# Which side of a subtraction is strided: the read or the write

## The chip, the cores and the metric

The kernel runs on one core of one Trainium2 chip. The metric is the device time of one execution in microseconds. Engines: TensorE (PE; its weight loads are PEld), VectorE (DVE), ScalarE (ACT), GpSimd (POOL), SyncE (SP, which only issues DMAs here).

## The reference

Attention over 8 batches, 8 heads, 576 tokens and 64 dimensions (a pooled part and a band of neighbours), followed by a dense layer. Only the dense layer matters here:

```python
def _moe_ref(x, w_in, w_out):          # x: 4608 x 512, w_in: 512 x 2048, w_out: 2048 x 512
    h = x @ w_in
    g = h - np.tanh(h)
    return (g @ w_out).astype(np.float32)
```

## The kernel before

One batch gives one block of 576 tokens. Its attention result lies in `xT` (features on partitions), with the tokens of a batch ordered as c, then g: token 4g + c, four classes c of G = 144. The dense layer takes the first 128 g of each c, so 512 tokens, as a block (`mm1`): 16 chunks of 128 hidden features, each four matmuls into one PSUM bank (line 782), tanh on ScalarE into the f32 tile `u` (line 794) and the subtraction on VectorE into the bf16 tile `gT` (line 797).

The last 16 g of each c, 64 tokens a batch, are the left tokens. They are done for two batches at once, four times in all (`left1(m, e)`, m = 0 to 3), in four groups e of four feature chunks: 16 matmuls of 128 columns each fill one PSUM bank (line 809); its 512 columns are, from outer to inner, chunk f (4), batch b (2), c (4) and g (16). Then tanh into `u` (line 820, the same order) and the subtraction into `gL` (line 822). `gL[:, f, :]` has 128 columns in the order of the tokens, b, g, c, since `left2` uses it as stationary operand (line 835) and stores its result in rows of tokens. So somewhere between the bank and `gL`, c and g change places, and the subtraction does it.

`u` is a ring of three buffers, and a bank or a buffer is free again when the subtraction has read it. `second` makes the second product (line 1003), which needs sums over `gT` that VectorE makes (line 938, the token sums); lines 691 (mask), 723 and 741 are VectorE's part of the attention of later batches, lines 491 to 562 bring q and k into their layouts: line 496 copies a transposed k out of PSUM with a changed order of elements, line 501 a transposed q in the same order, line 551 and line 557 pick q (and k) of a few tokens out of `rT`, line 562 reorders k inside SBUF. Line 410 casts v.

All instructions are put in one order written out by hand (`TURNS`), from which each engine's queue follows; an engine works its queue in order. Costs given to `op` (such as the 690 in line 822) change nothing in that order.

Of the kernel before, what the change touches and what calls it, by code (L numbers as in the profile page):

```python
# [10 lines left out]
ALU = mybir.AluOpType  # L11
# [3 lines left out]
class Plan:  # L15
# [13 lines left out]
    def op(self, eng, ns, fn, reads=(), writes=(), port=False, opens=None, uses=(),  # L29
           choice=None, rows=128, share=0.4):  # L30
        i = len(self.ops)
        deps = set()
        for key in reads:
            if key in self.last_write:
                deps.add(self.last_write[key])
        for key in writes:
            if key in self.last_write:
                deps.add(self.last_write[key])
            deps.update(self.readers.get(key, ()))
        for key in reads:  # L40
            self.readers.setdefault(key, set()).add(i)
        for key in writes:
            self.last_write[key] = i
            self.readers[key] = set()
        deps.discard(i)
        if opens and not isinstance(opens, list):
            opens = [opens]
        names = set(uses) | {o[0] for o in opens or ()}
        if choice:
            letter = self.engines[self.choices]  # L50
            self.choices += 1
            eng, ns, fn, port = next(a[:4] for a in choice if a[0][0] == letter)
        self.ops.append((fn, deps, opens or (), names))
        return i
# [34 lines left out]
def kernel(  # L89
# [125 lines left out]
    def fixed(name, shape, dt, n=None, pool=const):  # L215
        if n is None:
            return pool.tile(shape, dt, name=name, tag=name)
        return [pool.tile(shape, dt, name=f"{name}{i}", tag=f"{name}{i}")
                for i in range(n)]
# [39 lines left out]
    u = fixed("u", [128, 512], FP32, 3)  # L259
# [7 lines left out]
    gL = fixed("gL", [128, N_FF, 2 * LEFT], BF16)  # L267
# [4 lines left out]
    op = P.op  # L272
    V, A, T, GP = nc.vector, nc.scalar, nc.tensor, nc.gpsimd

    def at(name):
        c = P.place[name]
        return bank[:, c[0]:c[-1] + 1, :]
# [523 lines left out]
    def left1(m, e):  # L801

        name, us = ("hl", m, e), (2 * m * (N_FF + 2) + 2 * N_FF + e) % 3
        s0, f0 = m % 2, 4 * e

        def mm(fs):
            for f in fs:
                for dc in range(N_DC):
                    T.matmul(at(name)[:, 0, 128 * f:128 * f + 128],  # L809
                             w_in_sb[:, dc, (f0 + f) * 128:(f0 + f) * 128 + 128],  # L810
                             xT[dc].rearrange("p (b c g) -> p b c g", b=NR, c=4)[:, s0:s0 + 2, :, 128:G],
                             start=(f == 0 and dc == 0), stop=(dc == N_DC - 1),
                             skip_group_check=True)
        for n in range(2):
            op("PE", 432, lambda n=n: mm(range(2 * n, 2 * n + 2)),
               reads=[("w_in", e)] + [("xs", s0 + i, j) for i in range(2) for j in range(N_DC)],
               writes=[("hld", m, e)] + (["turn1"] if n == 0 else []),
               opens=(name, TAIL if m == NBLK // 2 - 1 else DENSE) if n == 0 else None,
               uses=[name])
        op("ACT", 600, lambda: A.activation(out=u[us], in_=at(name)[:, 0, :], func=AF.Tanh),  # L820
           reads=[("hld", m, e)], writes=[("u", us)], uses=[name])
        op("DVE", 690, lambda: V.tensor_tensor(  # L822
            out=gL[:, f0:f0 + 4, :].rearrange("p f (b g c) -> p (f b) c g", b=2, c=4),
            in0=at(name)[:, 0, :].rearrange("p (x c g) -> p x c g", c=4, g=16),
            in1=u[us].rearrange("p (x c g) -> p x c g", c=4, g=16), op=ALU.subtract),
           reads=[("hld", m, e), ("u", us)], writes=[("gL", e)],
           uses=[name])

# [274 lines left out]
    def dense(kb):  # L1103
        steps = iter(()) if kb == 0 else second(kb - 1)
        count = 0 if kb == 0 else 16 + 12 * SEVEN[kb - 1] + 4 * (kb % 2 == 0)
        done, most = 0, 16 + 4 * (kb % 2)
        for i in range(most):
            if kb < NBLK:
                if i < 16:
                    mm1(kb, i)  # L1110
                else:
                    left1(kb // 2, i - 16)
            while done < (i + 1) * count // most:
                next(steps, None)
                done += 1
        for _ in steps:
            pass
# [66 lines left out]
    for p in range(NPAIR):  # L1184
# [16 lines left out]
        if p % NP == NP - 1:  # L1201
            b = p // NP
# [41 lines left out]
```

## Time and profile before

| | |
|---|---|
| median of 3 runs | 324.93 us (322.91 to 326.27) |
| the profiled execution | 326.23 us, of it span 324.5 us |
| mean TensorE clock granted | 0.992 |
| line 822, subtraction for left tokens | 16 instructions, 20.1 us on VectorE |
| line 797, subtraction for blocks | 128 instructions, 83.8 us on VectorE |
| HBM traffic | 165 GB/s over the span |

An instruction group is named by line, engine and operation, output and inputs; the columns after it are the busy time in us, the mean time of one in ns, and the idle time of the engine just ahead of the group with what ended it. Lines that begin with a source line and give three times with slashes are minimum, median and maximum of one instruction in ns, then the first and last start. The chain of waits is the work that ended last, followed back from the end; its pieces have a start and a length in us.

### The profile page before, as it was taken

How to read it: one execution, taken by the hardware profiler on the slowest of the kernel's cores; microseconds unless marked ns; L12 is line 12 of the kernel's file. 1: busy time of each engine (PE TensorE's matmuls, PEld its weight loads, DVE VectorE, ACT ScalarE, POOL GpSimd, SP SyncE). 2: the span in 40 equal slices, each digit the busy share in tenths (PEclk: the TensorE clock that was granted, in tenths of full speed). 3: DMA queues.
4: the chain of work that ended last, by engine and by line, in shares of the span. 5: the costliest groups of instructions: out<-in, count | busy, mean ns of one | idle time of the engine just before them, and what ended most of it. 6: DMA issues, size and time to landing. Idle time of an engine off the chain costs nothing.

```text
span 324.5 us, 7865 instructions
## 1 busy us (share of the span) xinstructions
PE 307.2 (95%) x3014; PEld 200.3 (62%) x3014; DVE 271.2 (84%) x463; ACT 210.7 (65%) x380; POOL 175.2 (54%) x221
## 2 busy tenths in 40 slices
PE   8889999999997999999989999999999998999994
PEld 3574655454765665667577656755767467855583
DVE  3888885897998999999998798998997689746963
ACT  3897785677875787886755788477856773336410
POOL 5278973177684378647842968453914996500000
PEclk9999999999997999999999999999999999999999
DMA  7999999997996899987995897698947311440034
GB/s 221 262 271 233 251 220 182 250 234 177 264 280 158 132 275 262 292 172 194 223 242 167 188 243 162 183 239 160 335 112 131 86 46 51 74 147 0 2 97 129
DMA packets 114948, 59.62 MB, mean 184 GB/s; under 512 B 84064, under 2 KB 112224, under 8 KB 114912
## 3 DMA queue, kind: packets, MB, share of 16 engines
q1 hardware_dynamic: 109568, 52.77, 68.4%
q0 software_dynamic: 4704, 5.77, 9.7%
q10 hardware_dynamic: 640, 0.59, 0.6%
q8 instruction: 23, 0.38, 0.5%
q14 instruction: 13, 0.11, 0.1%
HBM read 44.04 MB, written 9.44 MB: 165 GB/s over the span
## 4 chain that ended last, share of the span: by engine, by line
PE 65%; DVE 15%; DMA 7%; ACT 4%; issue 4%; POOL 3%; SPq 1%; ACTq 0%; POOLq 0%; DVEq 0%
PE ps L782 29%; PE ps L1003 21%; DVE gL L822 5%; PE ps L705 4%; PE ps L863 4%; DMA w_in_sb<-in_moe_w_in_dram 3%; DVE gT L938 3%; PE ps L835 2%; DMA st<-in_q_dram 2%; PE ps L635 2%; DVE gT L797 2%; DMA sr<-in_k_dram 1%; DMA vst<-in_v_dram 1%; PE ps L809 1%; DVE S L938 1%
## 5 line engine op out<-in xcount | busy, mean ns | idle before, releaser
L782 PE MATMUL ps<-xT,w_in_sb 128*128 128x512 bf16 x512 | 123.0, 379 | 0.4 <-DVE xT L741 0.3
L797 DVE TENSOR_TENSOR gT<-ps,u 128x512 bf16<-128x512 f32 x128 | 83.8, 684 | 18.8 <-ACT u L794 17.8
L794 ACT ACTIVATE u<-ps 128x512 f32<-128x512 f32 x128 | 73.5, 598 | 38.5 <-PE ps L782 34.7
L1003 PEld LDWEIGHTS <-gT 128*128 128x128 bf16 x672 | 64.3, 98 | 21.3 <-DVE gT L938 5.1
L782 PEld LDWEIGHTS <-w_in_sb 128*128 128x128 bf16 x512 | 47.7, 98 | 47.8 <-issue 1.1
L1003 PE MATMUL ps<-Tw,gT 128*128 128x256 bf16 x336 | 43.5, 276 | 3.9 <-DVE gT L938 3.6
L1003 PE MATMUL ps<-w_out_sb,gT 128*128 128x256 bf16 x336 | 43.3, 273 | 1.2 <-DVE gL L822 0.8
L577 POOL TENSOR_TENSOR qkd<-half 128x288 bf16<-128x288 f32 x25 | 24.3, 972 | 27.4 <-DVE half L572 21.3
L484 POOL CAST qr<-st 128x512 bf16<-128x512 f32 x40 | 28.7, 724 | 15.3 <-DMA st<-in_k_dram 4.7
L656 ACT ACTIVATE E<-ps 128x912 bf16<-128x912 f32 x32 | 29.9, 935 | 2.7 <-PE ps L635 1.3
L723 DVE TENSOR_TENSOR ln<-ps,r 128x768 bf16<-128x768 f32 x32 | 30.6, 955 | 0.9
L572 POOL TENSOR_TENSOR half<-kq 128x576 f32<-128x576 bf16 x13 | 17.6, 1353 | 18.7 <-ACT kq L557 11.1
L1024 ACT COPY y<-ps 128x512 f32<-128x512 f32 x19 | 11.1, 586 | 24.0 <-PE ps L1003 23.9
L691 DVE TENSOR_TENSOR E<-E,mask 128x1152 bf16<-128x1152 bf16 x27 | 23.9, 886 | 3.2 <-ACT E L656 1.7
L705 PEld LDWEIGHTS <-E 128*128 128x128 bf16 x576 | 21.9, 98 | 5.8 <-DVE E L691 1.3
L1074 POOL TENSOR_TENSOR y<-y,keep 128x512 f32<-128x512 f32 x12 | 16.9, 1406 | 15.8 <-ACT y L1024 15.8
L664 ACT ACTIVATE E<-ps 128x576 bf16<-128x576 f32 x32 | 20.9, 652 | 6.9 <-PE ps L651 6.9
L562 ACT COPY kt<-kq 128x576 bf16<-128x576 bf16 x20 | 23.8, 1189 | 0.1
L822 DVE TENSOR_TENSOR gL<-ps,u 128x512 bf16<-128x512 f32 x16 | 20.1, 1310 | 1.2 <-ACT u L820 1.0
L705 PE MATMUL ps<-vw,E 128*128 128x65 bf16 x320 | 19.2, 195 | 0.6 <-DVE E L691 0.6
L938 DVE TENSOR_TENSOR gT<-gT 128x2048 bf16<-128x2048 bf16 x14 | 18.5, 1322 | 0.6 <-PE ps L1003 0.5
L741 POOL TENSOR_TENSOR xT<-lT 128x336 bf16<-128x336 bf16 (+1 forms) x24 | 16.6, 713 | 4.1 <-DMA lT<-ln 4.1
(122 smaller groups left out, 495.3 us busy)
## 6 DMA issues: line engine op xcount, KB each, us to landing
vst<-in_v_dram SPq DMA_DIRECT2D x64, 160.0 KB, 4.5
st<-in_k_dram SPq DMA_DIRECT2D x32, 256.0 KB, 3.4
st<-in_q_dram SPq DMA_DIRECT2D x32, 256.0 KB, 4.3
out_dram<-y SPq DMA_DIRECT2D x14, 512.0 KB, 3.0
v<-in_v_dram SPq DMA_DIRECT2D x14, 256.0 KB, 4.1
w_in_sb<-in_moe_w_in_dram POOLq DMA_DIRECT2D x4, 512.0 KB, 8.6
w_out_sb<-in_moe_w_out_dram POOLq DMA_DIRECT2D x4, 512.0 KB, 10.6
v<-in_v_dram POOLq DMA_DIRECT2D x6, 256.0 KB, 3.7
```

The source lines that it names most:

```text
L484: (eng, ns, lambda dst=dst, src=src, fn=fn: fn(out=dst, in_=src), port)
L577: eng.tensor_tensor(out=pooled, in0=half[:, 0:288].rearrange("p (n x) -> p n x", n=2), in1=half[:, 288:576].rearrange("p (n x) -> p n x", ...
L656: A.activation(out=E[s][:, :, E0:E0 + 456], in_=at(s1)[:, :, PS0:512], func=AF.Exp, scale=SCALE)
L691: eng.tensor_tensor(out=el, in0=el, in1=mask.unsqueeze(1).to_broadcast([128, 2, S]), op=ALU.mult)
L705: T.matmul(po[:, hh, 65 * n:65 * n + 65], E[s][:, hh, e:e + 128], vv, start=start, stop=stop)
L723: op("DVE", 960, lambda: V.tensor_tensor(out=ln[s].rearrange("p n (h d) -> p h n d", d=D), in0=blocks()[:, :, :, 0:64], in1=r[s].unsqueeze ...
L782: T.matmul(at(name)[:, 0, :], w_in_sb[:, dc, fc * 128:(fc + 1) * 128], xT[dc][:, c0:c0 + S].rearrange("p (c g) -> p c g", c=4)[:, :, 0:128 ...
L794: op("ACT", 600, lambda: A.activation(out=u[us], in_=at(name)[:, 0, :], func=AF.Tanh), reads=[("hd", kb, fc)], writes=[("u", us)], uses=[n ...
L797: op("DVE", 690, lambda: V.tensor_tensor(out=gT[g][:, fc, :], in0=at(name)[:, 0, :], in1=u[us], op=ALU.subtract), reads=[("hd", kb, fc), ( ...
L822: op("DVE", 690, lambda: V.tensor_tensor(out=gL[:, f0:f0 + 4, :].rearrange("p f (b g c) -> p (f b) c g", b=2, c=4), in0=at(name)[:, 0, :]. ...
L938: eng.tensor_tensor(out=dst[:, fs], in0=x0[:, fs], in1=x1[:, fs], op=ALU.subtract if sub else ALU.add)
L1003: T.matmul(dst, left[:, f, 128 * j:128 * j + 128], right[:, f, :], start=(first and e == 0 and f == 0 and (j == 0 or apart)), stop=(e == 1 ...
```

## The change

The subtraction walks its elements in the order f, b, g, c where it walked them as f, b, c, g. Before, the reads of PSUM and of `u` were side by side, and the write to `gL` (bf16) went in steps of four elements, 8 bytes. After, the write is side by side, and both reads (f32) go in steps of 16 elements, 64 bytes, four at a time, and then back. The values, the order of the instructions on each engine and all waits stay as they are.

```diff
         op("DVE", 690, lambda: V.tensor_tensor(
-            out=gL[:, f0:f0 + 4, :].rearrange("p f (b g c) -> p (f b) c g", b=2, c=4),
-            in0=at(name)[:, 0, :].rearrange("p (x c g) -> p x c g", c=4, g=16),
-            in1=u[us].rearrange("p (x c g) -> p x c g", c=4, g=16), op=ALU.subtract),
+            out=gL[:, f0:f0 + 4, :].rearrange("p f (b g c) -> p (f b) g c", b=2, c=4),
+            in0=at(name)[:, 0, :].rearrange("p (x c g) -> p x g c", c=4, g=16),
+            in1=u[us].rearrange("p (x c g) -> p x g c", c=4, g=16), op=ALU.subtract),
            reads=[("hld", m, e), ("u", us)], writes=[("gL", e)],
```

## The prediction, made before the change was run

> **What bounds the kernel now.** I read the busy shares first, then the costliest groups, then the chain of waits, then what TensorE waited for.
>
> ```profile
> PE 307.2 (95%) x3014; PEld 200.3 (62%) x3014; DVE 271.2 (84%) x463; ACT 210.7 (65%) x380; POOL 175.2 (54%) x221
> ```
>
> TensorE bounds the whole; VectorE is next. The changed line is line 822, the subtraction h - tanh(h) for the left tokens. Its twin is line 797, the same operation on the same number of elements with every operand side by side:
>
> ```profile
> L797 DVE TENSOR_TENSOR gT<-ps,u 128x512 bf16<-128x512 f32 x128 | 83.8, 684 | 18.8 <-ACT u L794 17.8
> L822 DVE TENSOR_TENSOR gL<-ps,u 128x512 bf16<-128x512 f32 x16 | 20.1, 1310 | 1.2 <-ACT u L820 1.0
> ```
>
> So the scattered write costs 1302 ns (median of the 16; 1310 is the mean) against 684. Is this time on the path? The chain of waits (start, length, piece) holds these pieces:
>
> ```profile
> 87.38 2.45 DVE gL L822 x2
> ...
> 94.45 1.22 DVE gL L822
> ...
> 163.91 2.11 DVE gL L822 x2
> ...
> 167.44 1.20 DVE gL L822
> ...
> 169.22 1.21 DVE gL L822
> ...
> 232.59 1.32 DVE gL L822
> ...
> 234.43 1.21 DVE gL L822
> ...
> 301.28 1.21 DVE gL L822
> ...
> 303.73 3.58 DVE gL L822 x3
> ```
>
> That is 13 of the 16, in four stages: 3, 4, 2 and 4 of them. TensorE's waits confirm it (total us, times, longest):
>
> ```profile
> PE ps L1003 <- DVE gT L938: 3.6, 4, 1.9
> ...
> PE ps L835 <- DVE gL L822: 1.2, 3, 0.5
> ...
> PE ps L1003 <- DVE gL L822: 0.8, 2, 0.5
> ...
> PE ps L809 <- DVE gL L822: 0.3, 1, 0.3
> ```
>
> The longest wait of the first row (1.9 us, before 100.73) belongs here too: VectorE runs almost without a gap from 87.38 to 100.6, three of the subtractions among its work, and TensorE waits for the token sum at the end of that run.
>
> **What the change removes: the scattered write.** Its price per element comes from rows with nothing strided: 512 elements take 684 ns (line 797), 768 take 955 (line 723), so 271/256 = 1.06 ns an element and 684 - 512 x 1.06 = 141 ns fixed. Line 822 runs at (1302 - 141)/512 = 2.27 ns an element. A write with its elements 8 bytes apart thus costs 1.21 ns an element.
>
> **What it adds: two strided reads.** One in four steps of 64 bytes from PSUM (`ps`), one the same way from SBUF (`u`), both f32. No row shows either at 64 bytes, so I bound each by the nearest rows:
>
> ```profile
> L496 DVE COPY kt<-ps x4: 681/692/693, 9.1 to 57.0; 128x512 bf16<-128x512 bf16 x4
> ...
> L551 ACT COPY kq<-rT x7: 298/307/314, 11.5 to 78.7; 128x64 bf16<-128x64 bf16 x7
> L551 DVE COPY kq<-rT x5: 208/210/453, 8.5 to 67.9; 128x64 bf16<-128x64 bf16 x5
> ...
> L557 ACT COPY kq<-rT x16: 414/422/440, 83.5 to 268.1; 128x128 bf16<-128x128 bf16 x16
> L557 DVE COPY kq<-rT x4: 258/266/272, 100.6 to 245.3; 128x128 bf16<-128x128 bf16 x4
> ...
> L562 ACT COPY kt<-kq x20: 1169/1186/1219, 89.6 to 268.7; 128x576 bf16<-128x576 bf16 x20
> ```
>
> PSUM: line 496 reads PSUM in steps of 256 bytes and writes side by side. It takes 692 ns for 512 elements, the time of line 797 (684). ScalarE tells the same: 588 ns for line 496, 589 for line 501, which reads side by side. I take the PSUM stride at nothing; the upper bound is the price of the strided write, 1.21 ns an element.
>
> SBUF: lines 551 and 557 read `rT` in steps of 16 bytes, line 562 reads `kq` in steps of 576 bytes, four at a time as the new code does with `u`. On ScalarE, lines 551 and 557 give (422 - 307)/64 = 1.80 ns an element, and lines 557 and 562 (1186 - 422)/448 = 1.71; side by side it does 0.84 ((935 - 598)/400, lines 656 and 794). On VectorE the pair gives (266 - 210)/64 = 0.88. A side-by-side SBUF copy there (line 410, 640 elements in 490 ns) runs at (490 - 141)/640 = 0.55, that is two elements per 1.1 ns; read the same way, the strided copy moves two per 1.75 ns. Three estimates, 1.71 to 1.80, for small and for large steps: I take 1.75 ns for each element of `u`. Lower bound: 1.06 (the stride is hidden, since one stream alone comes from SBUF); upper: 2.27, if short hops cost a read what they cost the write.
>
> New duration: 141 + 512 x 1.75 = 1037 ns (1017 to 1063 by the three estimates), 265 less than 1302. Bounds: 684 and 1302 from one strided read alone.
>
> Here a rule of the Trainium skill speaks against the change. Advanced Engine Details and Errata, SBUF Cachelines, says that an SBUF line has 16 bytes and that two hits on a line absorb the latency, while a new line at every access is penalised. The old write puts two elements in each 16 bytes and would be free, the new read of `u` takes a new line each time and would pay; by that rule the operation gets slower. The trace disagrees in its first half: the old write takes 1302 ns against 684.
>
> **What lies on the path, stage by stage.** The order of instructions stays the same on every engine, and no DMA, wait or semaphore is added. TensorE's idle times below are 0.16 us too short each, since the profile models a 512-column matmul at 379 ns while successive ones start 216 apart.
> - Stage 84 to 101: the first subtraction (85.91) is covered by the tanh that ends at 87.36. The other three shorten VectorE's run: 3 x 0.265 = 0.80, against a wait of TensorE of 1.90 + 0.16. Next late: still the token sum.
> - Stage 162 to 176: all four, 1.06. TensorE's waits here (0.53 before 166.44, 0.39 before 170.47) hold 1.24 with the correction, so 1.06 fits; next late is TensorE itself.
> - Stage 230 to 242: the first two, 0.53; the waits (0.25 and 0.23) hold 0.80. The last two already lie beside TensorE's work, which covers them: nothing.
> - Stage 298 to 309: one, then three behind the tanh of 303.10. That would be 1.06, but TensorE has 16 matmuls of 216 ns and 4 of 108 between 303.31 and 308.23, so it cannot finish before 307.2: 1.03.
>
> Sum 3.4 us. From it goes an overlap: three subtractions in a row take 3.58, 1.19 from start to start and not 1.30, while line 797 has 0.63 for 0.684. If the new form overlaps as little as line 797, each saves 0.20 between starts and not 0.265. Half of that doubt, 13 x 0.03 = 0.4, comes off: **3.0 us**. The later work follows: after each stage the chain returns to TensorE's matmuls. What could swallow the first 0.8 is the stretch from 126 to 138, where the chain crosses a DMA of `vst`.
>
> The profiled execution took 326.23 (span 324.5, 1.7 around it), so 323.2 on its own count. It was the slower end of the runs shown; on their median, 324.93, the forecast is 321.9.
>
> **Rivals.**
> 1. The read of `u` is hidden, because the engine waits for one SBUF stream only. For: lines 551 and 557 on VectorE rest on 56 ns. Against: ScalarE pays on three lines. Then 684 ns, 0.62 less each: stages 1.55 (the second tanh of the run ends at 88.24 and holds the third subtraction), 1.24, 0.80, 1.03 (the last three capped by the waits), 4.6 us: 320.3. Chance 13%.
> 2. Short hops cost a read as much as the write, 2.27 ns: 1302 ns again, no change, 324.9. For: the write shows that short hops can be dear; against: line 551's 16-byte steps are no dearer than line 562's. Chance 14%. The Trainium skill states something near this: Vector Engine (DVE) Microarchitecture Reference, 5.2 Measured stream behaviour on trn2, has 1.73 ns per column for one source hopping far at every element, but 2.50 for both sources, or the output alone, stepping 24 words. By the second figure an estimate is 1.42 us each and 1.6 us more in all; the old write at 2.27 lies under that figure, and no run so far shows the read.
> 3. Slower: the two strided streams do not run beside each other, and each costs what the strided write did. Place: the 13 subtractions on the chain. 141 + 512 x (1.06 + 2 x 1.21) = 1923 ns, 0.62 more each, 13 x 0.62 = 8.1 us: 333.0. It decides from 0.25 us more each (2.75 ns an element), which is 1%. For: both reads take steps of 64 bytes, unlike any row. Against: line 496 on two engines. Chance 8%.
> 4. The subtraction gets shorter and VectorE's run ends no sooner, because other pieces in it (the mask of line 691 at 97.65, 1.82 us long) wait or share a port. Then about 1 us is left: 323.9. Chance 3%.
>
> **How the numbers follow.** The forecast has 62%. About 1% (3.25 us) is what a measurement of this kernel can tell from no change, and 3.0 lies just under it with bounds of 2.5 and 3.4, so half of its chance counts as faster. Faster: 0.31 + 0.12 of rival 1 = 0.43. Slower: rival 3 and 0.02 of rival 2 = 0.10. Within 1%: 0.47. The range reaches from rival 1 less 0.5 (319.8) to no change plus 0.7, about half the spread of the runs (325.6); it leaves out rival 3 and the dear end of rival 2.
>
> **What would show it.** Line 822 at 1017 to 1063 ns: the SBUF price is right; near 684: hidden; at 1302 or more: short hops are dear; near 1900: the streams add. TensorE's waits for line 822 (1.2, 0.8 and 0.3 us) should shrink to under half, and the 1.9 us wait for the token sum to about 1.1. If line 822 comes out at 1037 and the time moves by under 1 us, the account of the stages is wrong.

## The result and the profile after

Over 20 runs each, the changed kernel has a median of 322.9 us (321.25 to 327.38) and the kernel before 326.35 us (322.49 to 331.39). The ratio is 0.9917, with a 95% interval of 0.9888 to 0.9947: 2.7 us less, between 1.7 and 3.7; it leaves out executions more than 1.5% above the fastest of their kernel, so it is not the ratio of the two medians, which take in all 20. The profiled executions are 322.18 us (span 320.4) after and 326.23 before, 4.05 apart; why that is more than the runs show is taken up below, with the kernels that change one stage or three.

From the busy shares and the groups of the changed kernel (columns as before):

```profile
PE 305.1 (95%) x3014; PEld 199.5 (62%) x3014; DVE 269.4 (84%) x463; ACT 210.5 (66%) x380; POOL 175.0 (55%) x221
...
L797 DVE TENSOR_TENSOR gT<-ps,u 128x512 bf16<-128x512 f32 x128 | 83.7, 683 | 16.7 <-ACT u L794 15.6
...
L822 DVE TENSOR_TENSOR gL<-ps,u 128x512 bf16<-128x512 f32 x16 | 15.9, 1016 | 1.4 <-ACT u L820 1.3
```

Line 822 fell from 1310 to 1016 ns (medians 1302 and 1015), its twin stayed at 683. The busy time saved is 4.2 us, the time 2.7. The chain of waits of the changed kernel shows what became of the 13 subtractions on it:

```profile
87.40 1.94 DVE gL L822 x2
...
93.69 0.93 DVE gL L822
...
159.38 3.57 PE ps L809 x64
163.41 1.47 PE ps L1003 x12
164.88 0.86 PE ps L835 x4
...
229.73 1.04 DVE gL L822
...
231.37 0.95 DVE gL L822
...
297.62 2.68 PE ps L809 x48
300.31 0.86 PE ps L835 x4
301.61 2.72 PE ps L835 x12
304.32 11.80 PE ps L1003 x108
```

Three are left in the first stage and two in the third. In the second and the fourth the chain now runs through TensorE alone, from line 809 through line 835 to line 1003. What TensorE waits for has changed with it:

```profile
PE ps L1003 <- DVE gT L938: 2.3, 3, 1.3
...
PE ps L748 <- DVE ln L723: 1.4, 1, 1.4
```

No wait of TensorE's matmuls for line 822 is listed any more (2.3 us before), and the waits for the token sums are 1.3 us less; in the first stage that wait is 0.24 us, where it was 1.90 (the longest left, 1.3, lies at 201.38). But there is a new wait of 1.4 us, of the transposes in line 748 for VectorE's line 723; it lies at 101.25, right behind the first stage. The largest piece of what made line 723 late stands in the timeline of VectorE (below it GpSimd's work of the same time):

```profile
98.09 1.34 DVE L557 COPY kq<-rT 128x128 bf16<-128x128 bf16 x1
...
97.59 1.71 POOL L572 TENSOR_TENSOR half<-kq 128x576 f32<-128x576 bf16 x1
```

Line 557 took 1.34 us beside GpSimd's addition; before the change the same copy took 0.26.

As TensorE's queue is the same in all kernels except the one that changes its matmuls, an execution can be compared with another by the start of the same matmul. So measured, from the first matmul of line 809 in each stage to a matmul behind it (for stage 1 that is the first matmul of stage 2, 60 us behind the stage, so that column holds all that lies between; minus is shorter):

```
us against the profile of before    stage 1    stage 2    stage 3    stage 4
(matmul it is measured to)          (161.74)   (173.52)   (237.14)   (319.91)
changed kernel                       -2.54      -0.88      -0.46      -0.89
forecast, before the overlap         -0.80      -1.06      -0.53      -1.03
```

In this execution 0.54 us came back between stages 2 and 3, and another 0.15 between 3 and 4. Stages 2 to 4 are a little below the account. Stage 1 shows three times its forecast.

### The profile page after: what moved, and what is told of

It reads as the page before. It is cut to its first block, busy times and chain, and to the rows that moved or that the text cites. A ratio compares the mean times of both kernels' runs of the same rounds, so it can differ in the third digit from the quotient of the medians.

```text
span 320.4 us, 7865 instructions
## 1 busy us (share of the span) xinstructions
PE 305.1 (95%) x3014; PEld 199.5 (62%) x3014; DVE 269.4 (84%) x463; ACT 210.5 (66%) x380; POOL 175.0 (55%) x221
## 4 chain that ended last, share of the span: by engine, by line
PE 72%; DVE 12%; DMA 7%; issue 2%; ACT 2%; SPq 2%; POOL 0%; ACTq 0%; DVEq 0%; POOLq 0%
PE ps L782 33%; PE ps L1003 20%; PE ps L863 4%; PE ps L705 3%; PE ps L835 3%; PE ps L809 3%; DMA w_in_sb<-in_moe_w_in_dram 3%; DVE gT L938 3%; PE ps L635 2%; DMA st<-in_k_dram 2%; DMA sr<-in_k_dram 2%; DVE E L691 2%; DVE gL L822 2%; DMA lT<-ln 1%; DVE xT L741 1%
## 5 line engine op out<-in xcount | busy, mean ns | idle before, releaser
L1003 PE MATMUL ps<-Tw,gT 128*128 128x256 bf16 x336 | 42.5, 273 | 2.6 <-DVE gT L938 2.3
L577 POOL TENSOR_TENSOR qkd<-half 128x288 bf16<-128x288 f32 x25 | 23.4, 937 | 26.3 <-DVE half L572 20.2
L1024 ACT COPY y<-ps 128x512 f32<-128x512 f32 x19 | 11.1, 585 | 22.1 <-PE ps L1003 22.0
L822 DVE TENSOR_TENSOR gL<-ps,u 128x512 bf16<-128x512 f32 x16 | 15.9, 1016 | 1.4 <-ACT u L820 1.3
```

The costliest lines, as they stand in the source:

```text
L577: eng.tensor_tensor(out=pooled, in0=half[:, 0:288].rearrange("p (n x) -> p n x", n=2), in1=half[:, 288:576].rearrange("p (n x) -> p n x", ...
L1003: T.matmul(dst, left[:, f, 128 * j:128 * j + 128], right[:, f, :], start=(first and e == 0 and f == 0 and (j == 0 or apart)), stop=(e == 1 ...
```

## Experiments

My theory at this point: the new price is the strided read of `u` from SBUF alone, PSUM's stride being free; and the gain comes to TensorE through the waits in stages 2 to 4. Rivals: both strided reads share the price; and the 2.5 us of stage 1 belong to the change.

**The tanh changes the order.** Only PSUM is read with a stride, by ScalarE and by VectorE; `u` is written and read side by side.

```diff
-        op("ACT", 600, lambda: A.activation(out=u[us], in_=at(name)[:, 0, :], func=AF.Tanh),
+        op("ACT", 600, lambda: A.activation(
+            out=u[us].rearrange("p (x g c) -> p x g c", c=4, g=16),
+            in_=at(name)[:, 0, :].rearrange("p (x c g) -> p x g c", c=4, g=16), func=AF.Tanh),
...
-            in1=u[us].rearrange("p (x c g) -> p x g c", c=4, g=16), op=ALU.subtract),
+            in1=u[us].rearrange("p (x g c) -> p x g c", c=4, g=16), op=ALU.subtract),
```

> Here the tanh reads its bank in steps of 64 bytes and writes u in the order of the tokens, so the subtraction reads u and writes gL side by side and only its read of PSUM is strided. If the stride in SBUF is the whole cost of the changed subtraction (my theory), line 822 falls from 1015 to about 684 ns and the tanh of line 820 stays at 597; the same if PSUM strides are free on ScalarE too. If the PSUM stride carries part of the cost, line 822 lands between 684 and 1015, and the tanh rises above 600. Time by the account of the stages: 1.2 to 1.9 us less than the changed kernel, 4 to 5 us less than before (ratio near 0.987); if TensorE's limits in stages 2 to 4 are wrong, up to 13 x 0.33 = 4.3 us less than the changed kernel.

Measured: 320.81 us, ratio 0.9892 (0.9835 to 0.9949). The subtraction (line 824 here) and the tanh, by minimum, median and maximum:

```profile
L824 DVE TENSOR_TENSOR gL<-ps,u x16: 675/680/692, 90.8 to 305.6; 128x512 bf16<-128x512 f32 x16
```

```profile
L820 ACT ACTIVATE u<-ps x16: 592/597/624, 89.8 to 304.8; 128x512 f32<-128x512 f32 x16
```

PSUM read in steps of 64 bytes costs neither engine anything: 680 ns is the time of line 797, and 597 is that of the tanh with side-by-side reads. The whole price of the new form is `u`. By the same matmuls, this kernel stands 1.26, 0.81 and 1.02 us below before in stages 2, 3 and 4. These are the limits that TensorE's waits had given for a subtraction of 684 ns (1.24, 0.80, 1.03).

**`u` alone is strided.**

```diff
-            in0=at(name)[:, 0, :].rearrange("p (x c g) -> p x g c", c=4, g=16),
+            in0=at(name)[:, 0, :].rearrange("p (x g c) -> p x g c", c=4, g=16),
```

> The subtraction reads PSUM side by side and u in steps of 64 bytes, four at a time; gL is written side by side. The elements subtracted do not belong together here, the work is the same. If u alone carries the cost: 1015 ns, as in the changed kernel. If the two strided reads add: well under 1015, for instance 850 if they share it evenly. One look, the time itself says nothing new (near 322 us).

```profile
L822 DVE TENSOR_TENSOR gL<-ps,u x16: 991/1014/1044, 85.0 to 301.7; 128x512 bf16<-128x512 f32 x16
```

1014 ns against 1015: the two strided streams do not add. The one execution took 321.67 us.

**The matmuls write the tokens' order.**

```diff
-                             xT[dc].rearrange("p (b c g) -> p b c g", b=NR, c=4)[:, s0:s0 + 2, :, 128:G],
+                             xT[dc].rearrange("p (b c g) -> p b g c", b=NR, c=4)[:, s0:s0 + 2, 128:G, :],
...
-            out=gL[:, f0:f0 + 4, :].rearrange("p f (b g c) -> p (f b) g c", b=2, c=4),
-            in0=at(name)[:, 0, :].rearrange("p (x c g) -> p x g c", c=4, g=16),
-            in1=u[us].rearrange("p (x c g) -> p x g c", c=4, g=16), op=ALU.subtract),
+            out=gL[:, f0:f0 + 4, :].rearrange("p f x -> p (f x)"),
+            in0=at(name)[:, 0, :], in1=u[us], op=ALU.subtract),
```

> Here the matmuls of line 809 read their moving operand xT in token order (c innermost, steps of 288 bytes), so PSUM, u and gL all have one order and nothing on ScalarE or VectorE is strided. Line 822 must then take 684 ns, as line 797 does; if it does not, something else than strides makes it dear. TensorE may pay: with a free stride line 809 stays at about 57 ns from start to start and the time is that of the kernel in which the tanh permutes; if each of the 256 matmuls took twice as long, 256 x 0.055 = 14 us more on a full engine, ratio near 1.03.

Measured: 370.98 us, ratio 1.1441 (1.138 to 1.1503). The subtraction takes 692 ns, as forecast for one without strides. TensorE pays far more than the dear case expected; its timeline in the first stage (start, length, group):

```profile
86.39 3.73 PE L809 MATMUL ps<-xT,w_in_sb 128*128 128x128 bf16 x16
```

Sixteen matmuls take 3.73 us where they took 1.06: 0.222 us from start to start against 0.056, that is 1.73 ns a column against 0.44. All 256 of them make 42 of the 46 us. TensorE's clock was also lower in this execution, 0.919 on the mean (the digits under 9 in this row of 40 equal slices, tenths of full speed):

```profile
PEclk9998999998599999999669999999579999997599
```

This does not make line 809's price: its matmuls start 0.223 us apart in the stretches with a granted clock of 0.50 (89.6 to 103.2 us is the first) and 0.223 outside them. It does lengthen the other matmuls: those in the four such stretches take 17.8 us from start to start, where the same ones took 11.1 before.

**Only the first stage, and only the other three.** The condition stands in all three patterns; the second kernel has `if m else`.

```diff
-            in1=u[us].rearrange("p (x c g) -> p x g c", c=4, g=16), op=ALU.subtract),
+            in1=u[us].rearrange("p (x c g) -> p x g c" if m == 0 else
+                                "p (x c g) -> p x c g", c=4, g=16), op=ALU.subtract),
```

> The changed subtraction in the first of the four stages alone; the other three write with a stride as before. In the profile of the changed kernel that stage gained 2.5 us by the start of the same matmul, where three subtractions 0.22 us shorter explain 0.7. Theory A: the shorter run of VectorE no longer meets GpSimd's next work, and the lengthening of the mask (1.82 us against 0.75) and of the sums beside it goes away; then this kernel alone has 2 to 2.5 us of the gain, ratio near 0.993. Theory B: the 1.8 us are chance of the executions profiled; then 0.7 us, ratio near 0.998, and the stage's landmarks in this profile move by 0.7.

> The changed subtraction in the last three stages alone; the first writes with a stride as before. By the account of the stages: 10 subtractions on the chain, 0.22 us each, 0.87 + 0.46 + 0.89 = 2.2 us, ratio near 0.993. Theory A leaves the first stage's long mask in place (1.2 to 1.9 us); under theory B the first stage may come out either way.

> The changed kernel once more, on the same chip as the others of this group, so that its parts add up against it: theory A 2.3 + 2.2 = 4.5 us less than before, ratio near 0.987; theory B 0.7 + 2.2 = 2.9 us, ratio near 0.991.

> The kernel in which the tanh permutes, on the same chip as the changed kernel. Its subtraction is 0.33 us shorter still. By the limits of TensorE in the stages: 0.4 + 0.35 + 0.14 = 0.9 us less than the changed kernel in stages 2 to 4, nothing further in stage 1. If TensorE did not limit those stages, 13 x 0.33 = 4.3 us less.

```
                                 median us   ratio to before (95%)      stage 1  2      3      4   (us)
first stage alone                324.19      1.001  (0.997 to 1.005)     -3.24   0.01  -0.01   0.01
stages 2 to 4 alone              322.12      0.9929 (0.9892 to 0.9967)   -2.57  -0.60  -0.46  -0.90
changed kernel                   322.21      0.9927 (0.9894 to 0.996)    -2.54  -0.59  -0.46  -0.89
tanh changes the order           320.35      0.9883 (0.9824 to 0.9942)   -2.84  -1.26  -0.81  -1.03
```

(Before in this group: 324.46 us, 28 runs. The stages are those of one profiled execution each, against the profile of before.)

Theory A falls. With the first stage changed alone, the time does not move, and with the others changed alone, it moves as far as in the whole change. Theory B's 0.998 lies within the interval of the first kernel, and so does no gain at all. The kernel that leaves the first stage as it was shows 2.57 us there too: so it was the profiled execution of before that was long. The clock does not make the difference between the kernels: over the executions in the ratios its mean was 0.997 before and 0.996 in both the changed kernel and the one with stages 2 to 4.

What made before long can be read from the two executions, which have the same instructions there. Before, VectorE's mask meets GpSimd's addition (timelines of VectorE and of GpSimd):

```profile
97.65 1.82 DVE L691 TENSOR_TENSOR E<-E,mask 128x1152 bf16<-128x1152 bf16 x1
...
97.15 1.71 POOL L572 TENSOR_TENSOR half<-kq 128x576 f32<-128x576 bf16 x1
```

In the kernel with the first stage unchanged, GpSimd was held by a DMA just then, and its work came behind the mask:

```profile
95.69 0.75 DVE L691 TENSOR_TENSOR E<-E,mask 128x1152 bf16<-128x1152 bf16 x1
...
97.57 0.61 POOL L484 CAST qr<-st 128x512 bf16<-128x512 f32 x1 [3.96 <-DMA kq<-qr]
98.15 1.27 POOL L572 TENSOR_TENSOR half<-kq 128x576 f32<-128x576 bf16 x1
```

Side by side, both are long (1.82 and 1.71); apart, both are short (0.75 and 1.27). In these two executions the DMA's landing decided it. Three other pieces of VectorE's run were longer too (line 379 with 1.22 for 0.69 us, two sums of line 938 with 0.98 and 1.27 for 0.69 and 0.68); the four make 2.5 us, and by the matmul at 100.73 the other execution is 2.71 ahead. Then TensorE's clock fell in before, to 0.52 from 101.0 to 104.5 us (the 7 in its row), and the lead grew to 4.30 by 105.92:

```profile
PEclk9999999999997999999999999999999999999999
```

Of it 1.7 us were lost again by 139.93, which leaves the 2.57. That the meeting with GpSimd is what lengthens the pieces was read from the traces and not tried by itself.

The kernel in which the tanh permutes is the fastest of the four; its ratio lies 0.0044 (1.4 us) under that of the changed kernel, and the landmarks of stages 2 to 4 give 1.2. The two intervals overlap, so its lead over the changed kernel is not settled by the runs; over the kernel before it is.

**What a step costs, in a write and in a read.** Five kernels, one execution each, with the pattern of one operand changed and all others side by side. Their elements land at other places than the reference's, or do not belong together, so they only time the step. The patterns of the operand in question:

```diff
write, 32 bytes
+            out=gL[:, f0:f0 + 4, :].rearrange("p f (b c g) -> p (f b) g c", b=2, c=4),
write, 16 bytes (4 bytes: c=2)
+            out=gL[:, f0:f0 + 4, :].rearrange("p f (x c) -> p (f x) c", c=8).rearrange(
+                "p (y x) c -> p y c x", y=8),
read, 8 bytes
+            in1=u[us].rearrange("p (y x c) -> p y c x", y=8, c=2), op=ALU.subtract),
read, 96 bytes
+            in1=u[us][:, 0:504].rearrange("p (x c) -> p c x", c=24), op=ALU.subtract),
```

> The subtraction reads PSUM and u side by side and writes gL (bf16) in steps of 32 bytes, four at a time, so every element goes to another 16 bytes; before the change the steps were 8 bytes, two elements to each 16. Elements land at other places than the reference's. If what costs is a new line of 16 bytes at each element, 32-byte steps cost at least as much as 8-byte steps: 1302 ns or more. If short hops are dearer than long ones: less than 1302, down to the price of the strided read, 1015.

> The subtraction reads side by side and writes bf16 in steps of 4 bytes, 32 at a time (the elements land at other places than the reference's). So far: 8-byte steps 2.27 ns an element, 32-byte steps (2348 - 141)/512 = 4.31. Theory L: a write costs 4.3 to 4.5 ns for each new 16 bytes that it touches, and 1.06 an element at least; four elements share 16 bytes here, so 1.1 ns each and about 700 ns. Theory H: the price grows with the hop; between 1.06 and 2.27 ns, 690 to 1302, for instance 1000.

> As above with steps of 16 bytes, 8 at a time. Theory L: one element to each 16 bytes, as with 32-byte steps: about 2350 ns. Theory H: between 8 and 32 bytes, for instance 3.3 ns an element, 1830 ns.

> The subtraction reads u (f32) in steps of 8 bytes, 32 at a time, everything else side by side (the elements subtracted do not belong together). With 64-byte steps the read costs 1.71 ns an element. If a read pays for each new 16 bytes as theory L has it for the write, two elements share the 1.71 and the time is that of a side-by-side read, 684 ns; if every element apart from its neighbour pays, about 1015 ns.

> The subtraction reads u (f32) in steps of 96 bytes, 21 at a time, 504 of the 512 elements (the other 8 are left out, gL is cleared at the start, and the elements subtracted do not belong together). If the price of a strided read is 1.71 ns an element whatever the step: 141 + 504 x 1.71 = 1003 ns. If steps of 96 bytes are dearer than those of 64, more. The Trainium skill (Vector Engine (DVE) Microarchitecture Reference, 5.2 Measured stream behaviour on trn2) has 2.50 ns per column for both sources stepping 24 words, by which an estimate is 1401 ns.

The three writes (4, 16 and 32 bytes) and the two reads (8 and 96 bytes), one kernel each:

```profile
L822 DVE TENSOR_TENSOR gL<-ps,u x16: 710/728/750, 87.1 to 301.4; 128x512 bf16<-128x512 f32 x16
```

```profile
L822 DVE TENSOR_TENSOR gL<-ps,u x16: 2390/2438/2681, 88.8 to 325.0; 128x512 bf16<-128x512 f32 x16
```

```profile
L822 DVE TENSOR_TENSOR gL<-ps,u x16: 2297/2348/2599, 89.4 to 323.1; 128x512 bf16<-128x512 f32 x16
```

```profile
L822 DVE TENSOR_TENSOR gL<-ps,u x16: 676/682/693, 86.2 to 299.5; 128x512 bf16<-128x512 f32 x16
```

```profile
L823 DVE TENSOR_TENSOR gL<-ps,u x16: 1252/1280/1298, 85.9 to 302.8; 128x504 bf16<-128x504 f32 x16
```

Less the fixed 141 ns, per element: writes 1.15, 2.27 (before the change, 8 bytes), 4.49 and 4.31 ns for 4, 8, 16 and 32 bytes; reads 1.06, 1.71 (64 bytes, four at a time) and 2.26 ns for 8, 64 and 96 bytes. Theory L holds for the write: 4.3 to 4.5 ns for each new 16 bytes, shared by the elements that lie in them; theory H does not, since 16 and 32 bytes cost about the same. The read at 8 bytes is free, as theory L has it, but its price for one element in 16 bytes depends on the pattern: 1.71 or 2.26, so "1.71 whatever the step" was wrong.

The long writes also show the path from the other side: at 2438 and 2348 ns the kernels took 347.24 and 345.25 us in one execution each, some 20 us more than before for 1.05 to 1.14 us in each of 16 subtractions. That is more than the 17 to 18 us that these add up to; the rest was not traced.

## Why the prediction was right

The forecast was 321.9 us on the median of the runs shown, a gain of 3.0; measured were 2.7, with an interval of 1.7 to 3.7 us, and a median of 322.9 in a range of 319.8 to 325.6. The price of the subtraction and stages 2 to 4 carried it; the term for stage 1 is not borne out, and that the sum still came within 0.3 us is partly luck.

- **The write's price** was read from the twin line, and `write_4B` to `write_32B` put it on a law that I did not have.
- **PSUM's stride at nothing**: right. The row that carried it (line 496, a copy of bf16 in steps of 256 bytes) held for f32 in steps of 64.
- **SBUF's stride at 1.75 ns**: 1.71, 1015 ns for the 1037 forecast, just under the band of 1017. The rows that carried it were reads of bf16 by two engines; VectorE's own gave 0.88, and its doubling to 1.75 was an argument that no run tested. The reason given, that small and large steps cost the same, was not right in general: steps of 96 bytes cost 2.26. The pattern here, four steps and back, happens to be that of line 562, whose 1.71 it shares.
- **Rival 1** (hidden read), **rival 3** (streams add) fell with `tanh_permutes` and `u_alone`. **Rival 2** (short hops as dear as in the write) fell for this pattern; the Trainium skill's 2.50 for 24 words (Vector Engine (DVE) Microarchitecture Reference, 5.2 Measured stream behaviour on trn2) is for both sources or for the output alone, and the one source here took 2.26 with that step, so a change with another pattern would have met it.
- **The rule on SBUF lines**, which spoke against the change, is half right. The Trainium skill (Advanced Engine Details and Errata, SBUF Cachelines) lets two hits on 16 bytes absorb the latency. The read agrees (682 ns with two elements to 16 bytes, more with one), the write does not (1302 with two, 728 with four).
- **Stages 2 to 4**: forecast 1.06 + 0.53 + 1.03 = 2.62 before the deduction; the landmarks give 2.23 and 1.94 in two executions, and stages 2 to 4 alone gave all of the gain in the runs (0.9929). The deduction for the overlap was too small: three subtractions in a row now start 0.92 us apart, where before they started 1.12 apart, so of 0.287 us in length only 0.19 counts. The prediction's 1.19 was not from start to start: it is a third of the 3.58 from the first start to the last end (and so is its 0.63 for line 797, whose starts lie 0.60 apart).
- **Stage 1** is the weak step: 0.80 was forecast, and with that stage changed alone the ratio is 1.001 (0.997 to 1.005), so at most 1.0 us gained and in the middle none. The 0.80 lies just inside the interval; the runs make it doubtful and do not exclude it. Single executions scatter as much: the kernel with this stage alone changed is 0.67 us shorter there than the one that leaves it alone, the changed kernel 0.03 longer. I had the VectorE run as one that ends sooner by what is taken out. That is where **rival 4** (3%) had a point: its other pieces grow and shrink with GpSimd and a DMA, by 2.5 us between two executions of the same code. In both executions of the changed kernel the mask was short (0.75), but GpSimd's addition then met lines 938 and 557 (1.34 for 0.26 us), and the wait of 1.90 us for the token sum turned into one of about 0.25 there and 1.4 for line 723 behind it. So the 0.80 may be swallowed in this way; how much of it is on the mean stays open.
- **The size of 1%**: the gain lies just under it, where the forecast put it.

The profile alone would have misled here. It shows 4.05 us, 2.5 of them in stage 1, with a neat mechanism at hand; the same stage in a kernel that leaves it unchanged shows 2.6.

## What to carry to other kernels

When a step must reorder its elements, let it do so where it reads PSUM: at the steps tried here (64 bytes in f32, 256 in bf16) that cost neither VectorE nor ScalarE anything, while the same reordering took 0.33 us more as a read of SBUF, 0.62 more as a write with two elements to each 16 bytes, and 1.73 ns a column instead of 0.44 in a matmul's moving operand. A saving on an engine that is not the bound is worth what its consumer waits for, stage by stage; those waits, lengthened by what the profile models off them, gave the gain of the best kernel to 0.02 us in each of three stages. And before a stage's gain is explained, look at the same stage in a kernel that leaves it alone.

## What the runs showed of the hardware

- VectorE's bf16 write to SBUF costs 4.3 to 4.5 ns for each new 16 bytes: 2348 ns for 512 elements at 32-byte steps, 2438 at 16, 1302 at 8, 728 at 4, 684 side by side. A strided f32 read at one element to each 16 bytes cost 1.71 or 2.26 ns, by its pattern.
- Three strided reads of SBUF on three engines cost about the same: 1.71 ns an element on VectorE (`u`, f32 in steps of 64 bytes), 1.71 to 1.80 on ScalarE (lines 551, 557, 562), 1.73 ns a column on TensorE (line 809 in steps of 288 bytes, at a granted clock of 0.50 as at 1.00). It is no rule for every pattern: VectorE's reads of `u` took 1.06 in steps of 8 bytes and 2.26 in steps of 96, and its bf16 copies of lines 551 and 557 took 0.88.
- VectorE's bf16 mask took 1.82 us beside a GpSimd addition and 0.75 apart from it, its copy of line 557 1.34 and 0.26; the addition took 1.71 and 1.27.
